# Eight single PSUM banks, first loads on other queues, and v products on GpSimd in a linear-attention and MLP kernel

## The chip, the core and the metric

The kernel runs on one core of a Trainium2 chip. Its time is the device time of one execution in microseconds (us): 360.28 is the median of three runs of the kernel before (359.89, 360.28 and 363.01). The core's engines work side by side, each through its own queue in order: TensorE (PE: matrix products and transposes into PSUM; its weight loads are listed as PEld), VectorE (DVE), ScalarE (ACT), GpSimd (POOL) and SyncE (SP, which here only asks for DMAs). An engine that reaches an instruction whose input is not there stands still, with everything behind it.

## What is computed

```python
def phi(x):                                   # x: 8 batches, 8 heads, 576 rows, 64 columns
    proj = einsum('bhsd,df->bhsf', x, w_phi)  # 128 features
    proj = proj - max(abs(proj), over f)
    return concatenate([exp(proj), exp(-proj)])
kv  = einsum('bhsf,bhsd->bhfd', phi(k), v);  z = sum over s of phi(k)
x   = einsum('bhsf,bhfd->bhsd', phi(q), kv) / (einsum('bhsf,bhf->bhs', phi(q), z) + 1e-6)
x   = x as 4608 rows of 8 heads x 64 = 512 columns
out = square(relu(x @ w_in)) @ w_out          # w_in 512 x 2048, w_out 2048 x 512
```

Inputs and output are float32; the products are made in bf16.

## The kernel before

**Two streams.** For each of 8 batches an attention part makes 4.5 tiles of 128 rows of `x`, 36 tiles in all. An MLP part takes them in chunks (`CHUNKS`: four of one tile, sixteen of two).

**Attention, a batch** (`k_batch`, `q_batch`). Keys are brought in with a cast to bf16, transposed (on PE for the first two batches, L630, by the DMA transpose after that), and projected with `w_phi` (L660) in five groups of 8, 8, 8, 8 and 4 blocks of 128 x 128. Of each group DVE takes the largest absolute value in a row (L595), and ACT makes exp of plus and of minus the projection (L602, tile `kph`). The row's maximum is applied on the side of v: ACT makes exp of it (`em`, L704), and `va` is v times that factor, eight blocks at a time (L755; `var` at L738 for the 64 rows that are left of a batch), with the factor itself as one more column (L716, L720). PE multiplies `kph` with `va` (L776, L781) into `kv`, copied to SBUF as `kvs`. For q there are two projections, one with rows on the partitions for the maximum (L878, reduced at L925) and one transposed (L888), from which ACT makes `qph` (L915). PE then forms numerator and denominator (L970, L978), DVE scales and adds the two halves (`tmp`, L1001 to L1019), takes the reciprocal (L1032) and multiplies (`xo`, L1042, L1046); `xo` is transposed into `xT`.

**MLP, a chunk** (`hp_chunk`, `op_chunk`). `hp` = `w_in` times `xT` (L1133) fills a bank of 512 columns at a time; relu takes it to SBUF (`hr`, L1151 on ACT or L1153 on DVE); it is squared from `hr` into `h2` (L1161 or L1163), one bank per instruction; `w_out` follows (L1189), a copy to `ot` and a DMA to `out`.

**PSUM.** There are 8 banks of 512 float32 columns. Ring `pj` holds three tiles of two banks each (projections, `kv` after the first batch, numerators); ring `mo` holds two single banks (transposes, the first batch's `kv`, `hp` and `op`). One reduction or one exp reads both banks of a `pj` tile: 1024 columns. In `after_kp` a lock keeps the reduction and the exps of the same tile apart in time.

**Order.** Every step is an `Op` with the engines that may do it, a cost, what it needs and what it holds. The table `ORDER`, made ahead of time, lists all steps in the order in which they are issued; a negative entry takes the second engine in the step's list. Each engine works in just that order. `WARM` adds matmuls on the identity ahead of some steps of PE; 24 on zeros (`WARM_UP`) open the kernel, and the step `fill` adds 40 (`FILL`) in the first batch. None of their results is read.

**First loads.** Keys of heads 0, 1, 4 and 5 come as float32 by SP's queue and are cast by ACT and DVE. GpSimd's queue asks, in this order, for the other heads of k, for v, then makes the identity, and asks for the rests of k and v, half of q, two parts of `w_in`, the other half of q, two more parts, the rest of q, batch 1's k, the two halves of `w_out` and batch 1's q and v. `w_phi` comes twice by ACT's queue, for partitions 0 to 63 and 64 to 127, into a tile of two column blocks.

Of the kernel before, what the change touches and what calls it, by code (L numbers as in the profile page):

```python
# [8 lines left out]
F32 = mybir.dt.float32  # L9
# [217 lines left out]
def kernel(  # L227
# [160 lines left out]
    def e_first(op):  # L388
        warm(r_pj.tile(op)[:, 0], WARM_UP, zero)
# [878 lines left out]
```

## Time and profile before

| what | value |
|---|---|
| time, median of three | 360.28 us |
| span of the profiled execution, first to last instruction | 358.4 us |
| its own time | not listed apart; the median stands 1.88 us above the span |
| busy: PE, DVE, ACT, POOL | 346.4, 292.4, 262.9, 58.5 us |
| chain of work that ended last: PE, DVE, ACT | 82%, 8%, 7% |
| mean granted TensorE clock | 0.990 |

The page of the profile has each engine's busy time, the span in 40 slices, and the chain of work that ended last. The table by windows gives the busy time of each engine in chosen stretches with the count of instructions in brackets, and the granted clock of TensorE (1.00 is full). The timeline lists instructions with their start, their length, and the idle time before them with what ended it. The groups by line and shape give the count, the busy time (overlaps counted once), and the mean length of one. Times count from the first instruction.

### The profile page before, as it was taken

The numbers are of one execution on the slowest core, as the hardware profiler recorded it, in microseconds if no ns is written. First come the engines' busy times: TensorE is split into PE (matmuls) and PEld (weight loads), VectorE is DVE, ScalarE is ACT, GpSimd is POOL, SyncE is SP. The second block draws the span as 40 slices with busy tenths as digits, with TensorE's granted clock in tenths as the row PEclk, the third lists the DMA queues.
The fourth block names the chain that finished last, engine by engine and source line by source line (L and its number), as shares of the span: only waits on it lengthen the run. The fifth ranks groups of instructions, "written<-read, shape, count | busy, mean of one in ns | idle before, by whom it ended". The sixth has DMA issues, their size and how long they took to land.

```text
span 358.4 us, 9254 instructions
## 1 busy us (share of the span) xinstructions
PE 346.4 (97%) x3860; PEld 239.1 (67%) x3894; DVE 292.4 (82%) x529; ACT 262.9 (73%) x436; POOL 58.5 (16%) x88
## 2 busy tenths in 40 slices
PE   8699999999999999999999999999999999999995
PEld 4378667775776676767576757757685768576754
DVE  5979998889998998788988699979988988591310
ACT  4979997996798774698849883798879867544641
POOL 8643323442160113100220002000000000000000
PEclk9969999999999999999999999999999999999999
DMA  9999999999997499607982194435203001113011
GB/s 161 185 197 207 194 208 141 170 181 187 186 152 138 83 171 150 107 15 145 124 126 53 59 149 96 61 89 82 60 16 88 18 35 48 65 34 88 2 59 59
DMA packets 92281, 39.33 MB, mean 110 GB/s; under 512 B 59728, under 2 KB 87760, under 8 KB 92240
## 3 DMA queue, kind: packets, MB, share of 16 engines
q0 software_dynamic: 42752, 18.09, 42.7%
q1 hardware_dynamic: 49328, 20.59, 28.6%
q8 instruction: 30, 0.49, 0.6%
q10 hardware_dynamic: 160, 0.07, 0.1%
q14 instruction: 11, 0.09, 0.1%
HBM read 36.77 MB, written 9.44 MB: 129 GB/s over the span
## 4 chain that ended last, share of the span: by engine, by line
PE 82%; DVE 8%; ACT 7%; issue 1%; POOL 1%; ACTq 0%; POOLq 0%
PE mo L1133 32%; PE mo L1189 31%; PE pj L781 4%; PE pj L970 4%; ACT kph L602 4%; PE pj L878 3%; PE pj L888 2%; DVE m L595 2%; PE pj L660 2%; DVE tmp L1009 1%; ACT hr L1151 1%; PE pj L776 1%; PE mo L781 1%; DVE va L755 1%; DVE hr L1153 1%
## 5 line engine op out<-in xcount | busy, mean ns | idle before, releaser
L1133 PE MATMUL mo<-xT,win 128*128 128x256 bf16 (+1 forms) x1280 | 139.3, 262 | 0.8 <-ACT hr L1151 0.2
L1189 PE MATMUL mo<-wout,h 128*128 128x512 bf16 (+1 forms) x558 | 131.2, 373 | 1.8 <-issue 0.2
L1133 PEld LDWEIGHTS <-win 128*128 128x128 bf16 x1280 | 111.3, 98 | 19.7 <-issue 4.3
L1189 PEld LDWEIGHTS <-h 128*128 128x128 bf16 x592 | 54.5, 98 | 57.3 <-issue 2.8
L915 ACT ACTIVATE qph<-pj 128x1024 bf16<-128x1024 f32 (+1 forms) x80 | 72.8, 940 | 11.6 <-PE pj L888 11.6
L1151 ACT ACTIVATE hr<-mo 128x512 bf16<-128x512 f32 x99 | 58.7, 598 | 28.2 <-PE mo L1133 27.0
L602 ACT ACTIVATE kph<-pj 128x1024 bf16<-128x1024 f32 (+1 forms) x80 | 71.2, 949 | 6.4 <-PE pj L660 4.9
L1163 DVE TENSOR_TENSOR h<-hr 128x512 bf16<-128x512 bf16 x82 | 33.7, 419 | 22.6 <-ACT hr L1151 22.0
L925 DVE TENSOR_REDUCE mq<-pj 128x8 f32<-128x1024 f32 (+1 forms) x40 | 44.2, 1108 | 4.5 <-PE pj L878 4.4
L595 DVE TENSOR_REDUCE m<-pj 128x8 f32<-128x1024 f32 (+1 forms) x40 | 44.3, 1111 | 3.4 <-ACT kph L602 1.7
L1161 ACT ACTIVATE h<-hr 128x512 bf16<-128x512 bf16 x62 | 38.9, 631 | 8.3 <-DVE hr L1153 7.5
L755 DVE TENSOR_TENSOR va<-vin,em 128x512 bf16<-128x512 bf16 x63 | 40.2, 683 | 0.1
L1153 DVE TENSOR_SCALAR hr<-mo 128x512 bf16<-128x512 f32 x45 | 30.6, 684 | 7.9 <-PE mo L1133 7.4
L417 ACT ACTIVATE ot<-mo 128x512 f32<-128x512 f32 (+1 forms) x24 | 14.0, 585 | 25.1 <-PE mo L1189 25.1
L1009 DVE TENSOR_TENSOR tmp<-pj,e 128x520 f32<-128x520 f32 x31 | 21.1, 692 | 6.1 <-PE pj L970 6.1
L970 PEld LDWEIGHTS <-qph 128*128 128x128 bf16 x512 | 21.9, 98 | 5.4 <-issue 1.5
L1042 DVE TENSOR_TENSOR xo<-tmp,rden 128x512 bf16<-128x512 f32 (+1 forms) x39 | 24.3, 631 | 0.5
L970 PE MATMUL pj<-kvs,qph 128*128 128x65 bf16 x512 | 24.4, 194 | 0.2
L781 PEld LDWEIGHTS <-kph 128*128 128x128 bf16 x512 | 21.5, 101 | 0.3
L1013 DVE TENSOR_TENSOR tmp<-pj,tmp 128x520 f32<-128x520 f32 x31 | 21.2, 692 | 0.5 <-PE pj L970 0.4
L781 PE MATMUL pj<-va,kph 128*128 128x65 bf16 x448 | 18.4, 194 | 0.0
L467 POOL DMA_DIRECT2D vin<-in_v_dram x8 | 7.2, 895 | 68.5 <-DVE va L755 63.1
(75 smaller groups left out, 268.5 us busy)
## 6 DMA issues: line engine op xcount, KB each, us to landing
out_dram<-ot SPq DMA_DIRECT2D x31, 256.0 KB, 2.4
vin<-in_v_dram POOLq DMA_DIRECT2D x8, 512.0 KB, 9.0
kin<-in_k_dram POOLq DMA_DIRECT2D x7, 512.0 KB, 11.9
qin<-in_q_dram POOLq DMA_DIRECT2D x7, 512.0 KB, 10.3
win<-in_moe_w_in_dram POOLq DMA_DIRECT2D x4, 512.0 KB, 10.1
wout<-in_moe_w_out_dram POOLq DMA_DIRECT2D x2, 1024.0 KB, 14.8
out_dram<-ot SPq DMA_DIRECT2D x10, 128.0 KB, 2.4
xT<-xo SPq DMA_TRANSPOSE x36, 2.6
```

The costliest lines, as they stand in the source:

```text
L595: nc.vector.tensor_reduce(out=st["m"].rearrange("p (n c) -> p c n", c=2)[:, :, n0 : n0 + n], in_=st["pj", g][:, :, :n], axis=AX.X, op=ALU. ...
L602: nc.scalar.activation(out=st["kph"][:, s, n0 : n0 + n].rearrange("p n c f -> p c n f"), in_=st["pj", g][:, :, :n], func=ACT.Exp, scale=1. ...
L755: nc.vector.tensor_tensor(out=st["va"][:, s, gs, 0:D], in0=tiles["v", b].rearrange("p h i d -> p (h i) d")[:, gs, :], in1=st["em"][:, s, g ...
L781: nc.tensor.matmul(out=kv[:, sum_of(h) - 2 * prs[0], :], lhsT=st["kph"][:, s, 2 * h + i // 2, i % 2, :], rhs=st["va"][:, s, h * NI + i, :] ...
L915: nc.scalar.activation(out=st["qph", pt][:, s, half, n0 : n0 + n], in_=in_, func=ACT.Exp, scale=1.0 - 2.0 * s)
L925: nc.vector.tensor_reduce(out=st["mq", pt][:, half, n0 : n0 + n], in_=in_, axis=AX.X, op=ALU.max, apply_absolute_value=True)
L970: nc.tensor.matmul(out=nps[:, n + 4 * (ab or 0), :], lhsT=qph[:, s, half, sl, :], rhs=kvs[:, s, sum_of(sl), :], start=True, stop=True)
L1133: nc.tensor.matmul(out=hp[:, mi, :], lhsT=win[:, kc, mc * P : (mc + 1) * P], rhs=st_x[c][:, kc, 0:nt, :], start=kc == kcs[0] and (ab is No ...
L1151: nc.scalar.activation(out=out_, in_=in_, func=ACT.Relu)
L1153: nc.vector.tensor_scalar(out=out_, in0=in_, scalar1=0.0, scalar2=None, op0=ALU.max)
L1161: nc.scalar.activation(out=out_, in_=hr, func=ACT.Square)
L1189: nc.tensor.matmul(out=st["op"], lhsT=hst["h2"][:, mc, tt * P : (tt + 1) * P], rhs=wout[:, mc, cols], start=(mc == 0), stop=(mc == KC2 - 1))
```

## The change

- **PSUM.** The rings `pj` and `mo` are gone. `r_ps` has eight single banks, for every step. Each projection takes two banks with a `Hold` each; reductions, exps, the additions into `tmp` and the copies of `kv` work on one bank each (512, 256 or 260 columns). In `after_kp` the lock holds one bank instead of two.
- **Counts.** Exps of `kph` and `qph` go from 80 and 80 to 160 and 160, the reductions on DVE from 80 to 160, the additions into `tmp` of full tiles from 62 of 520 columns (and 4 of 260) to 128 of 260.
- **Squares.** `hr` holds two banks, and one instruction squares 1024 columns (in all chunks but the last): ACT has 26 of 1024 and 4 of 512 instead of 62 of 512, DVE 42 and 4 instead of 82. Relus: 82 on ACT and 62 on DVE, instead of 99 and 45.
- **GpSimd.** `va_on` has GpSimd as a second engine, and so has the step of `xo`. In the new table 48 of the 64 products of `va` in all batches and 15 of the 16 of `var` stand on GpSimd, and 19 of the 41 of `xo`. In the first batch these are 6 of the 8 `va` and both `var`; ACT's eight small `va` instructions are gone. The columns of ones are copied by ACT or DVE.
- **First loads.** v of the first batch comes as float32 by SP's queue, in two halves, behind the keys and the rest of k, and stays float32 in a buffer of `h2`. The rest of k is cast by ACT. The identity is made ahead of GpSimd's first DMA. `w_phi` comes with one DMA that reads it twice, into a tile without column blocks. GpSimd's queue: other heads of k, rest of v, half of q, two parts of `w_in`, the other half of q, batch 1's k, two parts of `w_in`; then the eight products of the first batch; then the rest of q, batch 1's rest of k, the two halves of `w_out`, batch 1's q and v.
- **Later loads.** From batch 3 on they wait, on GpSimd, for a small copy from the first `xo` of the batch two before (`load_gate`, tile `mark`).
- **Fillers.** The 40 matmuls of `fill` are gone; `WARM` has other places, with 42 instead of 57.
- **Order.** A new table for 2084 steps instead of 1718.

The core of the diff, without the two tables and the changes of names:

```diff
-    r_pj = Ring("pj", 3, [P, 2, 4, P], F32, pool=ps)
-    r_mo = Ring("mo", 2, [P, 4, P], F32, pool=ps)
+    r_ps = Ring("ps", 8, [P, 4, P], F32, pool=ps)
-    r_hr = Ring("hr", 4, [P, 512], BF16)
+    r_hr = Ring("hr", 3, [P, 2, 512], BF16)
...
     def c_wst(_):
-        for half in range(2):
-            nc.scalar.dma_start(out=wst[half * Dh : (half + 1) * Dh], in_=w_phi)
+        nc.scalar.dma_start(out=wst, in_=w_phi.unsqueeze(0).to_broadcast([2, Dh, Fd]))
...
+            def emit_v(op, n=n):
+                if n == 0:
+                    tiles["v", 0] = r_h2.tile(op, [P, H, NI, D], dtype=F32)
+                nc.sync.dma_start(out=tiles["v", 0].rearrange("p h i d -> p h (i d)")[:, 4 * n : 4 * n + 4],
+                                  in_=v[0, 4 * n : 4 * n + 4, 0:SM, :].rearrange("h (p i) d -> p h (i d)", i=NI))
...
-            lock = Lock()
...
+            for par in range(2):
+                lock = Lock()
...
-        if b == 0:
-
-            def e_fill(op):
-                warm(r_mo.tile(op), FILL)
...
-            va_on = {"dve": (0.6, 0.69)}
+            va_on = {"dve": (0.6, 0.69), "pool": (1.0, 1.05)}
...
-                        nc.vector.tensor_tensor(
+                        eng = nc.gpsimd if op.engine == "pool" else nc.vector
+                        eng.tensor_tensor(
                             out=st["va"][:, s, gs, 0:D],
...
-                    o_xo = add(ks - 2.4, {"dve": dve(64 * (nh if ab is None else 4))}, e_xo, [o_rd],
+                    o_xo = add(ks - 2.4, {"dve": dve(n)} if first_tile else {"dve": dve(n), "pool": pool(n)}, e_xo, [o_rd],
...
-            def e_sq(op, mcs=mcs):
-                hr = st["hr", mcs[0]]
-                out_ = st["h2"][:, mcs[0] : mcs[-1] + 1, 0 : nt * P]
+            def e_sq(op, m0=m0, m1=mcs[-1] + 1, n=len(o_hrs)):
+                hr = st["hr", m0][:, :n].rearrange("p a (m t) -> p (a m) t", m=gm)
+                out_ = st["h2"][:, m0:m1, 0 : nt * P]
...
+    def load_gate(b, key):
+        o_xo, owner, st, name = firsts[b - 2]
+
+        def emit(_):
+            nc.gpsimd.tensor_copy(out=mark[:, b : b + 1], in_=st[name][:, 0, 0:1])
+
+        return add(key, {"pool": (0.1, 0.12)}, emit, [o_xo], give=[(r_xo.slots, owner)])
```

More of the change, by code (lines that the diff above doesn't have):

```diff
@@ L264 @@
     EARLY = 2
-    XB_IN, XB_X = 2, 2
+    XB_IN, PE_X = 2, [(b, pt, half) for b in range(2) for pt in range(3) for half in range(2)]
     def sum_of(h):
@@ L369, in c_w2 @@
     def c_w2(op):
-        for half in range(2):
-            rows = slice(half * Dh, (half + 1) * Dh)
-            copy(op, w2[rows, half], wst[rows])
+        copy(op, w2, wst)
     def c_wst(_):
-        for half in range(2):
-            nc.scalar.dma_start(out=wst[half * Dh : (half + 1) * Dh], in_=w_phi)
+        nc.scalar.dma_start(out=wst, in_=w_phi.unsqueeze(0).to_broadcast([2, Dh, Fd]))
     def c_var(_):
@@ L417, in copy @@
             nc.scalar.activation(out=out_, in_=in_, func=ACT.Copy)
+        elif op.engine == "pool":
+            nc.gpsimd.tensor_copy(out=out_, in_=in_)
         else:
@@ new lines, in k_batch, with e_kp @@
+        for g in groups:
+            key = kd - 6.0 - 2.2 * (4 - g)
+            holds = [Hold(r_ps.slots) for _ in range(2)]
+            def e_kp(op, g=g, holds=holds):
+                if g == 0:
+                    st["kph"], st["m"] = r_kph.tile(op), r_m.tile(op)
+                n0, n = GROUPS[g]
+                pj = [r_ps.tile(hold) for hold in holds]
+                st["pj", g, 0], st["pj", g, 1] = pj
+                warm(pj[0], op.warm)
+                for u in range(n):
+                    for par in range(2):
+                        rows = slice(par * Dh, (par + 1) * Dh)
+                        nc.tensor.matmul(out=pj[par][:, u, :], lhsT=st["kT"][rows, n0 + u, :], rhs=w2[rows, :],
+                                         start=True, stop=True)
+            o_kp = add(key - 1, {"pe": mm(P, GROUPS[g][1])}, e_kp, [cp_ops[g], o_w2],
+                       holds + ([r_kph.slots, r_m.slots] if g == 0 else []),
@@ L877, in e_qm @@
                             rows = slice(par * Dh, (par + 1) * Dh)
[L878 to L879 removed]
+                            nc.tensor.matmul(out=pj[bank][:, u, :], lhsT=q_blocks(st, pt, blk + u, 1)[rows, 0],
+                                             rhs=w2[rows, :], start=True, stop=True)
                 def e_qp(op, pt=pt, pi=pi, mms=mms, w=w, hq=hq):
[L882 removed]
+                    pj = st["pq", pt, pi] = [r_ps.tile(hold) for hold in hq]
@@ L907, in q_batch @@
-                if split and pi:
-                    late = o_qm, o_qp
-                o_mq, o_q0 = o_mq or o_qm, o_q0 or o_qp
-                for s in range(2):
-                    def e_exp(op, pt=pt, pi=pi, half=half, n0=n0, n=n, w=w, s=s):
-                        in_ = st["pq", pt, pi][:, :, :w]
-                        if n == 8:
-                            in_ = in_.rearrange("p a b t -> p (a b) t")
-                        nc.scalar.activation(out=st["qph", pt][:, s, half, n0 : n0 + n], in_=in_, func=ACT.Exp,
-                                             scale=1.0 - 2.0 * s)
-                    exps.setdefault(pi, []).append(add(key + 2.5 + 0.2 * s, {"act": act(size)}, e_exp, [o_qp],
-                                                       give=[(r_pj.slots, hq)]))
@@ L921, in e_red @@
-                def e_red(op, pt=pt, pi=pi, half=half, n0=n0, n=n, w=w):
-                    in_ = st["pm", pt, pi][:, :, :w]
-                    if n == 8:
-                        in_ = in_.rearrange("p a b t -> p (a b) t")
-                    nc.vector.tensor_reduce(out=st["mq", pt][:, half, n0 : n0 + n], in_=in_, axis=AX.X, op=ALU.max,
-                                            apply_absolute_value=True)
-                reds.append(add(key + (3.5 if b == 0 else 0.5), {"dve": dve(size)}, e_red, [o_qm], give=[(r_pj.slots, hm)]))
+                o_qm = add(key, {"pe": mm(P, w * (1 + split))}, e_qm, need + [o_w2], hm + first[:1], give=qT_give,
+                           after=[o_mq], mode="row")
@@ new lines, in q_batch, with e_exp, e_red @@
+                o_qp = add(key + (0.1 if b else 2), {"pe": mm(128 * w, 1 + split)}, e_qp, need + [o_w2], hq + first[1:],
+                           give=qT_give, after=[o_q0], mode="row")
+                o_mq, o_q0 = o_mq or o_qm, o_q0 or o_qp
+                mine = []
+                for bank, (half_, h0, nh_) in enumerate(banks):
+                    for s in range(2):
+                        def e_exp(op, pt=pt, pi=pi, bank=bank, half_=half_, h0=h0, nh_=nh_, w=w, s=s):
+                            nc.scalar.activation(out=st["qph", pt][:, s, half_, h0 : h0 + nh_],
+                                                 in_=st["pq", pt, pi][bank][:, :w], func=ACT.Exp, scale=1.0 - 2.0 * s)
+                        exps[half_, h0, s] = add(key + 2.5 + 0.2 * s, {"act": act(128 * w)}, e_exp, [o_qp],
+                                                 give=[(r_ps.slots, hq[bank])])
+                    def e_red(op, pt=pt, pi=pi, bank=bank, half_=half_, h0=h0, nh_=nh_, w=w):
+                        nc.vector.tensor_reduce(out=st["mq", pt][:, half_, h0 : h0 + nh_], in_=st["pm", pt, pi][bank][:, :w],
+                                                axis=AX.X, op=ALU.max, apply_absolute_value=True)
+                    mine.append(add(key + (3.5 if b == 0 else 0.5), {"dve": dve(128 * w)}, e_red, [o_qm],
+                                    give=[(r_ps.slots, hm[bank])]))
@@ new lines, in q_batch @@
+                            give = [(r_ps.slots, hold) for hold in holds]
+                            if s == 0:
+                                give.append((r_e2.slots, e2s[0]))
+                            at = ab or hg
+                            o_t[at] = add(ks - 3.5 + 0.5 * s, {"dve": dve(260) if pt < 2 else (0.85, 0.95)},
+                                          e_t, [o_nd, o_e2, o_t.get(at)], [] if o_tmp else [r_tmp.slots], give=give,
+                                          after=[o_tmp])
```

362 lines of the change are left out of this document (169 added, 193 removed), and 191 rows, old and new, of the table ORDER.

## The prediction

> **What bounds the kernel now.** I read the page first (busy times), then the table by windows, then the timeline of the start, the groups by shape, and the DMA issues. The page, and the table for the stretches before and after the first MLP matmul (28.41 us); its columns are PE, PEld, DVE, ACT and POOL with counts in brackets, then the granted clock:
>
> ```profile
> PE 346.4 (97%) x3860; PEld 239.1 (67%) x3894; DVE 292.4 (82%) x529; ACT 262.9 (73%) x436; POOL 58.5 (16%) x88
> ```
> ```profile
> 0.00:28.40 28.40, 23.21 (x250) 14.72 (x250) 22.40 (x45) 20.27 (x44) 18.25 (x32) 0.88 1.29 182
> 28.40:54.00 25.60, 24.86 (x357) 18.36 (x356) 25.38 (x49) 24.11 (x46) 7.95 (x11) 1.00 1.42 203
> 54.00:81.00 27.00, 26.37 (x373) 19.65 (x375) 22.56 (x43) 23.31 (x37) 11.28 (x16) 1.00 1.51 164
> 81.00:108.00 27.00, 26.79 (x328) 17.94 (x326) 26.34 (x44) 20.83 (x34) 8.25 (x12) 1.00 1.37 175
> 108.00:351.00 243.00, 241.42 (x2537) 165.44 (x2562) 195.75 (x352) 173.00 (x277) 12.77 (x18) 1.00 0.44 79
> 351.00:358.40 7.40, 3.76 (x34) 3.04 (x31) 0.00 (x0) 1.36 (x3) 0.00 (x0) 0.98 0.19 71
> ```
>
> TensorE is the bound. From 28.4 to 108 it is idle for 0.74 + 0.63 + 0.21 = 1.58 us, and from 108 to 351 for 1.58 of 243, at full clock. Faster work of any other engine there is worth 3.2 us at most, and the new program has the same matmuls, fillers apart. The end (from 351) is not touched. So the time is decided ahead of 28.4: whatever brings PE's dense stream forward moves the whole rest with it, as long as the inputs of that stream follow. The start:
>
> ```profile
> 3.62 0.42 ACT L417 ACTIVATE kin<-h 128x256 bf16<-128x256 f32 x1 [0.37 <-DMA h<-in_k_dram]
> 5.11 0.31 ACT L417 ACTIVATE w<-wst 64x128 bf16<-64x128 f32 x1 [0.87 <-DMA wst<-in_w_phi_dram]
> 5.73 0.42 DVE L419 COPY kT<-mo 128x512 bf16<-128x512 bf16 x1 [1.67 <-PE mo L630]
> 6.67 0.40 PE L660 MATMUL pj<-w,kT 64*128 64x128 bf16 x8
> 7.11 1.23 DVE L595 TENSOR_REDUCE m<-pj 128x8 f32<-128x1024 f32 x1 [0.75 <-PE pj L660]
> 8.36 2.85 ACT L602 ACTIVATE kph<-pj 128x1024 bf16<-128x1024 f32 x3 [0.34 <-DVE m L595]
> 9.07 2.33 PE L400 MATMUL mo<-ident 128*128 128x512 bf16 x10
> 11.09 0.33 ACT L704 ACTIVATE em<-m 128x16 f32<-128x16 f32 x2
> 17.14 0.67 ACT L602 ACTIVATE kph<-pj 128x512 bf16<-128x512 f32 x1
> 17.62 2.07 ACT L750 ACTIVATE va<-vin,em 128x64 bf16<-128x64 bf16 x8
> 19.52 2.00 ACT L915 ACTIVATE qph<-pj 128x1024 bf16<-128x1024 f32 x2
> 22.67 0.65 PE L781 MATMUL mo<-va,kph 128*128 128x65 bf16 x8
> 24.72 0.39 ACT L417 ACTIVATE kvs<-mo 128x260 bf16<-128x260 f32 x1 [0.88 <-PE mo L781]
> 28.41 1.79 PE L1133 MATMUL mo<-xT,win 128*128 128x128 bf16 x29
> ```
> ```profile
> 15.00:16.66 1.66, 0.00 (x0) 0.00 (x1) 1.62 (x4) 1.66 (x5) 1.00 (x3) 1.00 1.35 196
> 16.66:23.70 7.04, 7.04 (x82) 5.84 (x83) 6.00 (x10) 5.58 (x19) 3.25 (x5) 0.52 1.40 199
> ```
>
> The first exp waits until 8.36, although its projection began at 6.67: the lock lets it start only when DVE has reduced both banks (7.11 to 8.34). From there ACT's pieces follow each other to 21.52, the end of the first two `qph`. PE has nothing to do from 15.00 to 16.66, after which it runs at 0.52 of its clock until 23.70, busy all the time: kv is late because PE is slow there. The last `kvs` copy ends at 25.11, and 3.3 us later the MLP begins.
>
> **The change, part by part.** Lengths by shape:
>
> ```profile
> L602 ACT ACTIVATE kph<-pj 128x1024 bf16<-128x1024 f32 x64 | 62.9, 1034 | 6.4 <-PE pj L660 4.9 <-DVE m L595 1.3
> L602 ACT ACTIVATE kph<-pj 128x512 bf16<-128x512 f32 x16 | 9.2, 607 | 0.0
> L595 DVE TENSOR_REDUCE m<-pj 128x8 f32<-128x1024 f32 x32 | 38.8, 1218 | 3.4 <-ACT kph L602 1.7 <-PE pj L660 1.2
> L595 DVE TENSOR_REDUCE m<-pj 128x4 f32<-128x512 f32 x8 | 5.5, 683 | 0.1
> L1009 DVE TENSOR_TENSOR tmp<-pj,e 128x520 f32<-128x520 f32 x31 | 21.1, 692 | 6.1 <-PE pj L970 6.1
> L1001 DVE TENSOR_TENSOR tmp<-pj,e 128x260 f32<-128x260 f32 x2 | 0.8, 422 | 0.6 <-PE pj L970 0.6
> L755 DVE TENSOR_TENSOR va<-vin,em 128x512 bf16<-128x512 bf16 x63 | 40.2, 683 | 0.1
> L738 DVE TENSOR_TENSOR var<-vrest,em 64x512 bf16<-64x512 bf16 x16 | 11.0, 685 | 1.3 <-ACT em L704 1.0
> L1161 ACT ACTIVATE h<-hr 128x512 bf16<-128x512 bf16 x62 | 38.9, 631 | 8.3 <-DVE hr L1153 7.5
> L1151 ACT ACTIVATE hr<-mo 128x512 bf16<-128x512 f32 x99 | 58.7, 598 | 28.2 <-PE mo L1133 27.0
> L720 POOL CAST var<-em 64x8 bf16<-64x8 f32 x2 | 0.4, 214 | 1.1 <-ACT em L704 1.0
> ```
>
> *Evacuation by single banks.* An exp of 1024 columns takes 62.9/64 = 0.98 us of ACT, one of 512 9.2/16 = 0.575. Splitting 128 of them costs 2 x 0.575 - 0.98 = 0.17 each, 21 us; the 32 smaller ones add some 0.1 each, 3 us. Against it stand 17 relus fewer (58.7/99 = 0.59 each, -10 us) and squares merged: 26 of 1024 columns at about 0.98 and 4 at 0.63 are 28 instead of 38.9 us. ACT stays within 5 us of 263. On DVE, splitting 64 reductions costs 2 x 0.69 - 1.21 = 0.17 each, 11 us, the 62 additions 2 x 0.4 - 0.68 = 0.12 each, 7 us, and 17 relus come in; but 47 `va` (40.2/63 = 0.64 each, 30 us), 15 `var` (11.0/16 = 0.69, 10 us) and 19 `xo` leave it: DVE gets some 20 us lighter. Both have room beneath PE after 28.4, so I cost this at nothing there. If that cover fails, 5 us of ACT work in the full stretch 28.4 to 54 (24.11 of 25.60 busy) would cost some 3.
>
> *Start, up to the first exp.* `w_phi` needs one landing; before, the second copy ran only at 5.11. The keys land at the same 3.6; three casts on ACT (0.42 each, overlapping), the transposes and their copy (0.42 before) put the projection at about 5.45 instead of 6.67, and its end half a us later. ACT then takes the second bank while DVE reduces the first. First exp: 5.95 instead of 8.36, -2.4 us.
>
> *ACT's chain to qph.* From 8.36 to 19.52 before. The sixteen exps of 512 and four of 256 need about 0.8 more than the ten before; new on ACT are the cast of k's rest (0.4) and four copies of ones (0.2 each, like `em`, 0.33 for two); gone are the eight `va` (2.07); I add 0.8 for waits on DVE's reductions. So 19.52 - 2.4 + 0.8 + 0.4 + 0.8 - 2.07 + 0.8 = 17.85.
>
> *GpSimd's products.* No product on GpSimd is in the trace. From below: its 64x8 cast takes 0.21, so a product is over that, say 0.5 with 64 times the columns. From above: twice DVE's 0.68, and one collision with a DVE product of 0.68: 2.05. I take the 1.05 that the kernel's own table of costs has, since the same table has 0.6 to 0.69 for DVE's `va`, and the trace 0.68. The first factor `em` comes after nine exps and the cast, 5.95 + 4.45 = 10.4; product one until 11.45, the second needs the rests' factor (about 12.05), the eight end at 12.05 + 7 x 1.05 = 19.4. The last kv (0.65 at half clock, twice) then ends at about 20.9, ahead of the ACT instruction that copies it, so they are hidden behind ACT. [...]
>
> *First MLP matmul.* From 17.85 ACT has two exps, `e`, a `kvs` copy, five exps and the last `kvs` copy: 7 x 0.575 + 0.2 + 2 x 0.39 = 5.0, less 0.5 for overlap back to back: 22.3, instead of 25.11. Then the old 3.3, less 0.4 for the first half's additions that no longer stand behind it: 25.2. That is -3.2. If PE is again at half clock in this stretch (the 40 fillers that kept it busy from 9.07 to 11.40 are gone), the few matmuls between are inside those 2.9. [...] Bounds: 23.5 if GpSimd and PE never make it wait (-4.9), and 27.5 if ACT's chain gains nothing beyond the first exp's lead less its new work (-0.9).
>
> *More done by then.* The new order has 12 transposes, 2 matmuls of 512 columns more and 8 of 65 fewer ahead of the first MLP matmul. At 1.79/29 = 0.062 for 128 columns: 12 x 0.062 + 8 x 0.062 - 8 x 0.031 = 1.0 us, -1.0.
>
> *After 28.4.* Of the 1.37 us that PE is idle to 81 I take half back, -0.7, since DVE, which is full there (25.38 of 25.60), loses products to GpSimd.
>
> *What is late next: `w_out`.*
>
> ```profile
> L477 POOL DMA_DIRECT2D krest<-in_k_dram x16 | 10.1, 639 | 12.5 <-DMA kT<-krest 5.8 <-DMA qin<-in_q_dram 4.8 <-DMA win<-in_moe_w_in_dram 0.9
> 19.93 0.89 POOL L531 DMA_DIRECT2D wout<-in_moe_w_out_dram  x1 [0.90 <-DMA qin<-in_q_dram]
> 22.52 0.88 POOL L531 DMA_DIRECT2D wout<-in_moe_w_out_dram  x1 [1.69 <-DMA win<-in_moe_w_in_dram]
> DMA to landing us min/median/max: 13.4/14.8/16.1
> L1189 PE MATMUL mo<-wout,h x37: 379/379/390, 40.1 to 57.1; 128*128 128x512 bf16 x37
> ```
>
> It is now queued on GpSimd behind the eight products and four small issues (0.64 each): 19.4 + 2.6 = 22.0 instead of 19.93. It lands 13.4 to 16.1 later, 35.4 to 38.1. PE's first use of it stands 11.2 us of matmuls behind the first MLP matmul: 25.2 + 11.2 = 36.4. Between a gain of nothing and a stall of 1.7 I take +0.8. Batch 1's q and v are queued behind it and slip with it by about 2 us; what hides that is the MLP work of the first chunks, and if it does not, those 2 us are the price. Squares over two banks make `h2` ready up to a relu and half a square later (0.9 us); four to eight banks in flight hide that.
>
> *Sum.* -3.2 - 1.0 - 0.7 + 0.8 = -4.1: a span of 354.3, and with the 1.9 by which the median (360.28) stands above the profiled span (358.4), 356.2 us.
>
> **Rivals.** *ACT eats the lead (same).* ACT is on the path from 8.4 to 21.5 without a gap, and it gets 2 us of new work there. If splitting ten exps costs the whole 0.17 each, and PE's clock drops earlier because the fillers are gone, kv ends where it did; the MLP starts at 27.5, less 1.0 for the work done ahead, plus a late `w_out`: 358.5 to 360. For it: the half clock came after a PE gap of under 2 us; against it: the waits of the lock are gone for sure. I take 359.
>
> *GpSimd becomes the chain (slower).* With products of p us the eight end at 10.4 + 8p or so, kv 1.5 later, the MLP 3.9 after that as now. Up to p = 1.5 the start is no later than 28.4; from there each 0.1 costs 0.8, and `w_out`, issued 2.6 after them, slips as much. At p = 2.05 the products end at 26.8 and the MLP starts at 32.2: +3.8, less 1.0, with 1.0 for `w_out` (landing at 44 on the mean, used at 43.4) and 1.0 for waits of later batches: 358.4 + 4.8 + 1.9 = 365.1 us. For it: nothing in the trace shows a product there, and DVE works in SBUF beside it all the time. Against it: ACT and DVE are planned around 1.05.
>
> **How the numbers follow.** Forecast (356.2, own range 353 to 357.5): 0.58. ACT eats the lead (359): 0.25. GpSimd the chain (365): 0.17. A measurement of this kernel tells about 1%, 3.6 us, from no change. Faster by more is below 356.7: the forecast less 0.04 for its upper tail, 0.54. Slower is above 363.9: the last rival less 0.03 for products that only just pass 1.5, 0.14. Same is the rest: 0.04 + 0.25 + 0.03 = 0.32. The range goes from 353.0 (start at 23.5: 358.4 - 4.9 - 1.0 - 1.4 and no late `w_out`, + 1.9) to 362.0, which leaves out most of the last rival and a little of the forecast below.
>
> **What would show it.** Right: first exp of `kph` near 6.0; the first MLP matmul at 24 to 26; PE over 97% busy behind it; GpSimd's products near 1.05; the first `w_out` matmul waiting less than 2 us. Wrong: products over 1.5, kv waiting for POOL, PE waiting for DMAs of batch 1, or an ACT that is the releaser of most PE waits beyond 28.

## The result, and the profile after

The changed kernel takes 381.7 us (median of four runs, 379.4 to 382.39) against 360.08 of the kernel before on the same chip: a ratio of 1.0575, 95% interval 1.053 to 1.062, 21.6 us slower. The prediction was 356.2 with a range to 362. The profiled execution of the changed kernel took 382.39 us, with a span of 380.6 (before: 358.4).

The page of the changed kernel (busy times, the granted clock in 40 slices, the chain of waits):

```profile
PE 353.7 (93%) x3888; PEld 244.9 (64%) x3888; DVE 284.8 (75%) x566; ACT 257.0 (68%) x559; POOL 145.8 (38%) x170
PEclk9669997999999999699999999999999999999999
PE 60%; DVE 20%; DMA 7%; ACT 5%; issue 3%; SPq 2%; POOL 1%; DVEq 0%; ACTq 0%; POOLq 0%
```

DVE's share of the chain went from 8% to 20% and DMA now has 7%, although DVE is busy 7.6 us less. Two slices in the middle show a clock of 6 and 7 tenths, where the kernel before had none. The table by windows, of the changed kernel and then of the kernel before (columns as in the prediction):

```profile
54.00:81.00 27.00, 23.16 (x324) 16.99 (x324) 21.98 (x47) 19.53 (x45) 12.93 (x18) 0.87 0.63 90
130.00:160.00 30.00, 25.73 (x267) 15.85 (x266) 17.62 (x38) 15.70 (x36) 12.44 (x17) 0.91 1.08 148
28.40:380.60 352.20, 331.56 (x3652) 230.21 (x3650) 263.80 (x527) 237.55 (x509) 122.30 (x138) 0.98 0.61 97
```
```profile
28.40:358.40 330.00, 323.20 (x3613) 224.43 (x3644) 270.03 (x485) 242.61 (x393) 40.25 (x57) 1.00 0.67 104
```

Behind 28.4 us PE is idle for 352.2 - 331.56 = 20.6 us, before for 6.8. That is 13.8 of the 22.2 us by which the span grew. The other 8.4 us are longer busy time. Two stretches of 6.8 us at a granted clock of 0.50 make up 5.6 of it by an estimate that takes half of the 5.12 and 6.14 us that PE is busy in them (a matmul of 256 columns took 0.22 us of busy time from 154.65 to 161.48, 0.13 from 162 to 175 at full clock); the rest would be work of the start, whose first MLP matmul comes 1.8 us later.

```profile
55.67:62.49 6.82, 5.12 (x41) 3.22 (x41) 5.86 (x12) 1.79 (x5) 3.13 (x3) 0.50 0.77 147
154.65:161.48 6.83, 6.14 (x28) 3.78 (x28) 1.29 (x2) 5.17 (x11) 0.00 (x0) 0.50 1.26 203
```

These stretches are those of one execution. The four executions had mean granted clocks of 0.963, 0.976, 0.977 and 0.987 and took 382.39, 381.76, 379.4 and 381.64 us, so the time hardly followed the clock, and what the half rate costs is open.

Ahead of the first stretch stands one gap of PE. The timeline of the changed kernel there:

```profile
51.27 1.05 POOL L781 TENSOR_TENSOR va<-vin,em 128x512 bf16<-128x512 bf16 x1 [4.08 <-ACT em L730]
51.32 1.05 DVE L438 CAST va<-em 128x16 bf16<-128x16 f32 x1
52.26 3.06 DVE L438 CAST var<-em 64x8 bf16<-64x8 f32 x2
52.26 0.95 POOL L511 DMA_DIRECT2D vin<-in_v_dram  x1
53.22 1.05 POOL L763 TENSOR_TENSOR var<-vrest,em 64x512 bf16<-64x512 bf16 x1
53.51 0.40 PE L1092 MATMUL ps<-ident,xo 128*128 128x128 bf16 x4
54.23 1.04 POOL L781 TENSOR_TENSOR va<-vin,em 128x512 bf16<-128x512 bf16 x1
55.44 1.54 DVE L781 TENSOR_TENSOR va<-vin,em 128x512 bf16<-128x512 bf16 x1
56.90 0.41 DVE L438 COPY qT<-ps 128x512 bf16<-128x512 bf16 x1
57.37 1.87 PE L1213 MATMUL ps<-wout,h 128*128 128x512 bf16 x4 [3.46 <-DVE qT L438]
```

Three casts of a few columns take DVE from 51.32 to 55.32, while GpSimd makes products and, from 52.26 on, issues a DMA. The chain of waits has the last of them by itself:

```profile
52.44 2.88 DVE var L438
```

This one cast lasts until GpSimd has ended the two products that follow the DMA's issue. Behind the casts in DVE's queue stands the copy of `qT` for which PE waits 3.46 us (53.91 to 57.37), and 1.8 us into that gap the clock drops. The groups by shape, changed kernel first, then the kernel before:

```profile
L781 POOL TENSOR_TENSOR va<-vin,em 128x512 bf16<-128x512 bf16 x42 | 47.1, 1143 | 40.2 <-ACT em L730 24.7 <-issue 14.7 <-DMA vin<-in_v_dram 0.5
L781 DVE TENSOR_TENSOR va<-vin,em 128x512 bf16<-128x512 bf16 x14 | 12.3, 888 | 0.7 <-issue 0.6
L438 DVE CAST var<-em 64x8 bf16<-64x8 f32 x6 | 5.4, 898 | 0.0
L438 DVE CAST va<-em 128x16 bf16<-128x16 f32 x5 | 3.4, 683 | 0.0
L438 DVE CAST va<-em 128x64 bf16<-128x64 f32 x2 | 2.2, 1089 | 0.0
```
```profile
L720 DVE CAST var<-em 64x8 bf16<-64x8 f32 x14 | 2.7, 194 | 0.1
L716 DVE CAST va<-em 128x64 bf16<-128x64 f32 x6 | 1.8, 303 | 0.0
L716 DVE CAST va<-em 128x16 bf16<-128x16 f32 x8 | 1.5, 236 | 0.0
```

The same casts take 194 to 303 ns before and 683 to 1089 after. So the first theory: a GpSimd product and a DVE instruction that works in SBUF alone keep each other out ("the lock" from here on, not the one in `after_kp`); DVE, which works in order, passes the delay on to PE, and the fixed order has no slack for it. The rivals: the new table with its single banks is slow by itself (theory 2, later rival 1); or DMAs land late (theory 3).

### The profile page after: what moved, and what is told of

Read it like the earlier page. It is cut to its first block, busy times and chain, and to the rows that moved or that the text cites. A ratio compares the mean times of both kernels' runs of the same rounds, so it can differ in the third digit from the quotient of the medians.

```text
span 380.6 us, 9564 instructions
## 1 busy us (share of the span) xinstructions
PE 353.7 (93%) x3888; PEld 244.9 (64%) x3888; DVE 284.8 (75%) x566; ACT 257.0 (68%) x559; POOL 145.8 (38%) x170
## 3 DMA queue, kind: packets, MB, share of 16 engines
q0 software_dynamic: 41168, 17.50, 38.9%
## 4 chain that ended last, share of the span: by engine, by line
PE 60%; DVE 20%; DMA 7%; ACT 5%; issue 3%; SPq 2%; POOL 1%; DVEq 0%; ACTq 0%; POOLq 0%
PE ps L1142 26%; PE ps L1213 20%; PE ps L804 4%; DMA xT<-xo 4%; PE ps L978 3%; DVE m L634 3%; DVE tmp L1013 2%; ACT kph L642 2%; DMA qin<-in_q_dram 2%; DVE mq L929 2%; SPq L1077 2%; DVE hr L1170 2%; DVE tmp L1020 2%; PE ps L898 2%; DVE h L1186 2%
## 5 line engine op out<-in xcount | busy, mean ns | idle before, releaser
L1142 PE MATMUL ps<-xT,win 128*128 128x256 bf16 (+1 forms) x1280 | 141.2, 266 | 5.5 <-DMA xT<-xo 3.6
L1213 PE MATMUL ps<-wout,h 128*128 128x512 bf16 (+1 forms) x592 | 135.5, 375 | 4.9 <-DVE qT L438 3.5
L922 ACT ACTIVATE qph<-ps 128x512 bf16<-128x512 f32 (+1 forms) x160 | 79.5, 570 | 16.1 <-PE ps L908 16.0
L642 ACT ACTIVATE kph<-ps 128x512 bf16<-128x512 f32 (+1 forms) x160 | 79.5, 573 | 10.0 <-PE ps L699 8.1
L1168 ACT ACTIVATE hr<-ps 128x512 bf16<-128x512 f32 x82 | 48.7, 604 | 32.8 <-PE ps L1142 25.8
L1170 DVE TENSOR_SCALAR hr<-ps 128x512 bf16<-128x512 f32 x62 | 41.7, 682 | 28.5 <-PE ps L1142 27.9
L781 POOL TENSOR_TENSOR va<-vin,em 128x512 bf16<-128x512 bf16 x42 | 47.1, 1143 | 40.2 <-ACT em L730 24.7
L634 DVE TENSOR_REDUCE m<-ps 128x4 f32<-128x512 f32 (+1 forms) x80 | 47.8, 627 | 5.6 <-ACT kph L642 3.7
L929 DVE TENSOR_REDUCE mq<-ps 128x4 f32<-128x512 f32 (+1 forms) x80 | 46.8, 626 | 5.8 <-PE ps L898 5.5
L1186 DVE TENSOR_TENSOR h<-hr 128x1024 bf16<-128x1024 bf16 (+1 forms) x46 | 33.7, 735 | 8.3 <-ACT hr L1168 7.7
L434 ACT ACTIVATE ot<-ps 128x512 f32<-128x512 f32 (+1 forms) x22 | 13.0, 589 | 28.4 <-PE ps L1213 22.0
L804 PEld LDWEIGHTS <-kph 128*128 128x128 bf16 x512 | 21.6, 101 | 1.6 <-issue 1.4
```

Of the source, the lines that this page charges most:

```text
L634: nc.vector.tensor_reduce(out=st["m"].rearrange("p (n c) -> p c n", c=2)[:, par, n0 : n0 + n], in_=st["pj", g, par][:, :n], axis=AX.X, op= ...
L642: nc.scalar.activation(out=st["kph"][:, s, n0 : n0 + n, par, :], in_=st["pj", g, par][:, :n], func=ACT.Exp, scale=1.0 - 2.0 * s)
L781: eng.tensor_tensor(out=st["va"][:, s, gs, 0:D], in0=tiles["v", b].rearrange("p h i d -> p (h i) d")[:, gs, :], in1=st["em"][:, s, gs].uns ...
L804: nc.tensor.matmul(out=kv[:, sum_of(h) - 2 * prs[0], :], lhsT=st["kph"][:, s, 2 * h + i // 2, i % 2, :], rhs=st["va"][:, s, h * NI + i, :] ...
L922: nc.scalar.activation(out=st["qph", pt][:, s, half_, h0 : h0 + nh_], in_=st["pq", pt, pi][bank][:, :w], func=ACT.Exp, scale=1.0 - 2.0 * s)
L929: nc.vector.tensor_reduce(out=st["mq", pt][:, half_, h0 : h0 + nh_], in_=st["pm", pt, pi][bank][:, :w], axis=AX.X, op=ALU.max, apply_absol ...
```

## The experiments

The kernel before ran beside each group of these: 359.8 to 360.9 us. Each fence of a diff shows the core of an edit.

**The lock by itself.** A small kernel of its own, in three stretches: DVE and ACT instructions alone, GpSimd's products alone, and both.

```diff
+    for _ in range(100):
+        product(0)          # GpSimd, 128 x 512, float32 factor broadcast
+    for _ in range(8):
+        nc.vector.tensor_copy(out=ones[:, :, 64], in_=em[:, 0:16])
...
```

> None of the reference's work is done; the output is zeros. Eight each of nine kinds of DVE instruction and two of ACT, first alone, then beside a row of 100 GpSimd products of 128 x 512 (float32 factor broadcast, bf16 out), with eight of these alone between. Theory 1: beside GpSimd the DVE kinds that read and write SBUF alone (casts of ones, va product, squares) get up to one GpSimd product longer (the casts from 0.2 to about 1 us), or GpSimd's products get longer in their turn; those that read PSUM (relu, reductions, kT copies, additions to tmp) stay as they are, and so do ACT's. Rival (the casts were long in the changed kernel for another reason, such as a wait that the trace puts into the length): all kinds within 10% of their length alone.

Its groups; the smaller line number of each pair is the kind alone:

```profile
L63 DVE CAST ones<-em 128x16 bf16<-128x16 f32 x8 | 1.6, 202 | 0.2
L98 DVE CAST ones<-em 128x16 bf16<-128x16 f32 x8 | 8.7, 1086 | 0.2
L65 DVE TENSOR_TENSOR va<-vin,em 128x512 bf16<-128x512 bf16 x8 | 5.6, 694 | 0.2
L100 DVE TENSOR_TENSOR va<-vin,em 128x512 bf16<-128x512 bf16 x8 | 10.6, 1322 | 0.2
L67 DVE TENSOR_TENSOR h<-hr 128x1024 bf16<-128x1024 bf16 x8 | 5.5, 692 | 0.2
L102 DVE TENSOR_TENSOR h<-hr 128x1024 bf16<-128x1024 bf16 x8 | 11.4, 1428 | 0.2
L73 DVE TENSOR_SCALAR relu<-bank 128x512 bf16<-128x512 f32 x8 | 5.5, 690 | 0.2
L108 DVE TENSOR_SCALAR relu<-bank 128x512 bf16<-128x512 f32 x8 | 5.5, 690 | 0.2
L80 ACT ACTIVATE relua<-banka 128x512 bf16<-128x512 f32 x8 | 4.8, 597 | 0.3
L114 ACT ACTIVATE relua<-banka 128x512 bf16<-128x512 f32 x8 | 4.8, 595 | 0.2
```

The casts of 16 columns get 0.88 us longer, products and squares 0.63 and 0.74, each less than one GpSimd product alone (1.12). Everything that reads PSUM (relus 690 ns in both, reductions 689 and 690, copies 423 and 422, additions 426 and 427), ACT (597 and 595, squares 1055 and 1056), and a reciprocal in float32 (202 ns in both) stay as they were. GpSimd's products take 1.28 us each while DVE's instructions run beside them, 1.12 ahead of that and 1.02 behind it, with DVE idle. Theory 1's mechanism is there, in that both sides take longer. What it is that the two share, no run shows; `port`, in the kernel a mark of steps of `va`, `var`, `xo` and the squares, is no more than a name for it.

**The products back on DVE, order kept.**

```diff
+            if o.engine == "pool" and "dve" in o.engines:   # all; or va and var only; or xo only
+                o.engine = "dve"
```

> The changed kernel with all 82 products of va, var and xo on DVE; the order table, the eight banks and the loads stay. DVE gets 48 x 0.64 + 15 x 0.69 + 12 x 0.68 + 7 x 0.42 = 52 us of work more. Theory 1 (a GpSimd product and a DVE instruction that works in SBUF alone keep each other waiting, and DVE's queue then holds up PE): the casts of ones fall from 0.9 to 0.2 us, the half clock at 55 and 154 us is gone, and the time is 360 to 368, although DVE has 52 us more. Theory 2 (the single banks and the new order are to blame, the products' engine is not): DVE is only fuller, 382 to 392. Theory 3 (late DMAs: the transposes of xo at 150 us, v and w_phi at the start): 376 to 384, with the wait of 6.5 us on xT still there.

> The changed kernel with the 63 products of va and var on DVE, xo's 19 still on GpSimd. Theory 1: the stall of 3.5 us at 52 us and its half clock go, as the casts and var were the instructions held up there; 366 to 374. Theory 2: 380 to 390. Theory 3: as now, 378 to 384.

> The changed kernel with the 19 products of xo on DVE, va and var still on GpSimd. Theory 1: xo's products are 18 of GpSimd's 89 us of products, so a fifth of the loss goes at most: 374 to 381; if the chain through xo and its transposes at 120 to 160 us is what counts, 370. Theory 2: 381 to 386. Theory 3: 378 to 384.

Measured: 428.7, 418.9 and 404.4 us (ratios 1.193, 1.163, 1.121, each within 0.008). All far outside what the theories expected. Theory 1 is wrong in one part: to clear GpSimd is no cure while the table stays. DVE is busy 315.2, 306.8 and 295.6 us instead of 284.8, that is 30, 22 and 11 more, and the kernel takes 47, 37 and 23 more. In this order a microsecond added to DVE costs about 1.5 to 2.1 (the added work stands net of the lock that goes). The table was made for GpSimd's products running beside DVE. If it has no room for these products, it has none either for what the lock adds; that is an inference, which the later experiments test.

**Idle products in the kernel before.** This separates the lock from the table: nothing moves, GpSimd only makes products that nobody reads.

```diff
+                        if b >= 2: dummy(st["em"][:, s, gs])
...
+        nc.gpsimd.tensor_tensor(out=scratch["b"], in0=scratch["a"], in1=em.unsqueeze(2).to_broadcast([P, 8, D]), op=ALU.mult)
```

> The kernel before with nothing moved, but beside each of DVE's 48 va products of batches 2 to 7 GpSimd makes a product of the same shape from the same factor into a tile that nobody reads. [...] Theory 1: DVE's va and casts get longer by up to 0.6 each beside it, 20 to 30 us in sum; DVE has some 45 us of room from 108 to 351, so the time grows by 3 to 20: 363 to 380. Rival 1 (the lock is real but a queue absorbs it): 359 to 362.

> The kernel before with the same 48 idle GpSimd products of batches 2 to 7, each over one column in 64 (8 elements a row instead of 512, about 0.25 us). The control for the 47 us that the full ones cost: same instructions, waits on em and releases of em, but little time in the port. Theory 1 (the lock): the loss shrinks nearly with the length, 359 to 368. Rival (a GpSimd reader of em holds buffers or delays DMA issues): 385 or more.

Measured: 408.1 us (ratio 1.132, 1.127 to 1.137) with full products, 361.6 (1.003, 1.0005 to 1.005) with one column in 64. Groups of the first:

```profile
L581 POOL TENSOR_TENSOR dummyb<-dummya,em 128x512 bf16<-128x512 bf16 x48 | 59.8, 1246 | 148.8 <-ACT em L706 145.9
L757 DVE TENSOR_TENSOR va<-vin,em 128x512 bf16<-128x512 bf16 x63 | 56.1, 935 | 0.7 <-DMA vin<-in_v_dram 0.5
L740 DVE TENSOR_TENSOR var<-vrest,em 64x512 bf16<-64x512 bf16 x16 | 18.8, 1176 | 1.3 <-ACT em L706 1.0
L718 DVE CAST va<-em 128x64 bf16<-128x64 f32 x6 | 7.5, 1252 | 0.0
```

And its table of PE's waits (us in total, times, longest):

```profile
PE pj L779 <- DVE var L740: 6.8, 1, 6.8
PE mo L1136 <- DVE hr L1156: 6.6, 1, 6.6
```

DVE's own `va` went from 40.2 to 56.1 us, `var` from 11.0 to 18.8, the casts of 64 columns from 1.8 to 7.5; DVE is 38.9 us busier in all, and PE waits up to 6.8 us at a time for it. The kernel is 47 us longer, where at most 20 had been expected, for work that no step needs, and nearly all of that goes when the products are short. So the lock costs time in the old order too; it needs no new table.

**What the lock is worth in the changed kernel.** GpSimd's products cut to one column in 64 (`va` and `var`; then `xo` too), and the casts of ones moved to ACT.

```diff
-                            out=st["va"][:, s, gs, 0:D],
+                            out=st["va"][:, s, gs, 0:1 if op.engine == "pool" else D],
...
+            if op is a copy of ones:   # the other experiment
+                o.engine = "act"
```

> The changed kernel, engines and order untouched, but the 63 products of va and var on GpSimd write one column of 64 (the other 63 keep what a memset at the start, 2 us on DVE, put there), so 63 parts in 64 of those products are left out; a product falls from 1.14 to some 0.2 us. In the measured run the DVE kinds that work in SBUF alone were some 17 us longer in sum than alone (casts of ones 8, va 3, squares 3, xo 2, var 1). Theory 1 as it stands now (in this table DVE's queue has no room: 10.8 us more of DVE work cost 22 us with xo on DVE, 22 us cost 37 with va and var there; GpSimd's lock adds some 15 us to DVE): most of the 15 go, and the time falls to 355 to 366. Rival 1 (the table and the single banks are bad by themselves, whatever GpSimd does): 375 to 384. Rival 2 (it is the length of GpSimd's products that kv waits for, not the lock): also 355 to 366, but then the casts on DVE are no shorter in it than now.

> The changed kernel with all 82 products on GpSimd, xo's too, cut to one column in 64 (the rest left out), and the tiles behind them filled once at the start. With va and var cut it was 372. If the 18 us of xo's products, in the port and on the path from tmp to the transposes, are what is left: 362 to 367. If what is left is the table itself (single banks, more instructions, transposes too close to their use): 369 to 373.

> The changed kernel with the casts of the ones columns (13 on DVE, 11.0 us there, 0.9 each instead of 0.2) on ACT, which the single measurement shows untouched by GpSimd; ACT gets 13 x 0.25 = 3.3 us. Theory 1: DVE is 11 us lighter, at 1.3 or more per us: 364 to 372, and the PE gap at 57 us shrinks or goes. Rival 1: 378 to 386, since ACT is no emptier than DVE.

Measured: 372.3 us (ratio 1.034, 1.031 to 1.037), 371.9 (1.031, 1.027 to 1.034) and 375.5 (1.043, 1.039 to 1.047). The first and the third lie between the ranges of theory 1 and rival 1, the second in that of the table itself. The products of `va` and `var` cost 9.4 of the 21.6 us, those of `xo` nothing (by the intervals such a difference is good to about 2 us). Moving thirteen small casts to ACT alone brings 6.2, and the gap at 57 us goes with them: PE is busy 26.38 us from 54 to 81 instead of 23.16. That the casts shrink with the products (the 64 x 8 ones to 204 ns) speaks for the lock and against mere length. But some 12 us stay, so rival 1 or the DMAs have a part.

**The loads of a batch beside transposes.** In the changed kernel, and also with the products cut or the casts on ACT, PE stood still, and then ran at half clock, between 140 and 162 us (3.7, 3.6 and 3.9 us of waiting for a copy into `ot`, a granted clock of 0.91, 0.89 and 0.89 from 130 to 160).

```diff
-            nc.gpsimd.tensor_copy(out=mark[:, b : b + 1], in_=st[name][:, 0, 0:1])   # no gate
...
+            if (name, b) == ("k", 5): nc.gpsimd.tensor_copy(out=mark[:, 0:2], in_=st_x[8][:, 2, 1, 0:128:64])   # late5
```

> The changed kernel without the small copy that holds back the loads of batches 3 to 7; they go as soon as GpSimd's queue and the input buffers let them. In every variant so far two transposes of xo at about 140 us and the output DMA between them take 6 to 8 us to land, while GpSimd, released by that copy at 138 us, has just asked for k, the rests and q of a batch; PE stands still for 3.7 us there and loses some 3.4 us more at half clock. Theory 4 (the gate bunches the loads onto those transposes; a second cause beside the lock): 372 to 377. Rival (the transposes are late anyway, or the loads only collide elsewhere): 380 to 386.

> The ones columns on ACT and no gate, together; the whole computation is done. If the two causes add up: 375.5 less 5 to 8: 367 to 371. If the gate is not a cause: 374 to 379.

> Products of va and var on GpSimd cut to one column in 64 (63 parts in 64 of them left out), and no gate. If the lock and the gate are the two causes of the loss, what is left is xo's 18 us on GpSimd and the start: 362 to 367. If something else of the table (single banks, squares) is behind the rest of the loss: 370 to 374.

Measured: 383.7, 378.7 and 375.8 us, 2 to 3.5 more than with the gate in each case. This experiment could not decide: without the gate batch 5's k was still asked for at the same moment (138.5 us against 138.9, in the pair with cut products). Ahead of it in GpSimd's queue stands a product of `xo`, which itself starts only at 137.72 after 16.61 us of waiting. So the edit took away a wait that was not the last one, and told nothing about the meeting of loads and transposes. The next edit holds the loads until the transposes have landed.

> As with va and var cut to one column (372.3; 63 parts in 64 of these products are left out), and batch 5's loads, asked for at 138 us, held until both transposes of the rest tile of xo have landed (a copy of two elements of that tile on GpSimd ahead of them). If the transposes land late because the loads share the DMA engines with them: they land in 3 to 4 us instead of 6 to 7, the wait of 3.6 us at 147 and the half clock behind it go, 364 to 368, unless batch 5's keys are then late. If they are late without the loads: 371 to 375.

> The ones columns on ACT (375.5) and the same hold on batch 5's loads; the whole computation is done. If the loads delay the transposes: 367 to 371. If not: 374 to 378.

> The changed kernel with nothing but the hold on batch 5's loads until the transposes of the rest tile of xo have landed. With the ones columns on ACT, and with va and var cut, the hold gave 3.0 and 4.0 us. If it stands by itself beside the lock: 377 to 380 for the changed kernel. If the lock shifts the meeting of loads and transposes: 381 to 384.

Measured: 368.3 us (ratio 1.021, 1.018 to 1.024), 372.5 (1.032, 1.027 to 1.038) and 377.4 (1.047, 1.044 to 1.051): 4.0, 3.0 and 4.3 us less than without the hold. The first two lie between the ranges set for them, the third in the range of a cause beside the lock. The timelines of GpSimd, SP and PE, changed kernel and then with the hold:

```profile
145.69 0.94 POOL L511 DMA_DIRECT2D kin<-in_k_dram  x1
148.11 3.15 SPq L1077 DMA_TRANSPOSE xT<-xo  x2
155.22 0.61 PE L908 MATMUL ps<-qT,w 64*128 64x512 bf16 x2 [3.72 <-ACT ot L434]
```
```profile
147.32 2.45 SPq L1078 DMA_TRANSPOSE xT<-xo  x2
150.93 0.19 POOL L509 COPY mark<-xT 128x2 bf16<-128x2 bf16 x1 [5.99 <-DMA xT<-xo]
```

The chain of waits of the changed kernel there, and the window from 130 to 160 with the hold:

```profile
150.04 6.49 DMA xT<-xo
156.56 3.57 PE ps L1142 x16
```
```profile
130.00:160.00 30.00, 29.68 (x352) 20.28 (x350) 22.85 (x51) 20.57 (x45) 10.58 (x15) 1.00 0.85 127
```

Beside the loads a transpose lands 6.5 us after its issue ended, and PE goes on with it at 156.56. The gap of 3.72 us just ahead is for a copy into `ot`, whose buffer an output DMA still held; with the products cut, the chain of waits names the one that SP had issued between the transposes, 6.8 us long. With the hold both have landed at 150.93, when the copy that waits for them starts, 1.2 us after the second was issued (147.32 + 2.45). PE is then busy 29.68 of 30 us at full clock from 130 to 160, instead of 25.73 at 0.91. So the loads here delay what lands beside them (6.5 us against 1.2), and that is a second cause beside the lock. Part of the gain is given back later (PE is busy 36.91 us from 160 to 200 instead of 39.22, with 1.5 us of waiting for the rest of k, which now comes later).

**Instructions split over single banks**, in the kernel before, with its order.

```diff
-                nc.vector.tensor_reduce(... in_=st["pj", g][:, :, :n], ...)
+                for c in range(2): nc.vector.tensor_reduce(... in_=st["pj", g][:, c, :n], ...)   # exps and tmp likewise
```

> The kernel before with its own order and rings, but each exp, each reduction and each addition into tmp that reads two banks made as two instructions, one for each bank, as in the change. DVE gets 64 x 0.17 + 62 x 0.12 = 18 us, ACT 64 x 0.17 + 64 x 0.17 + 3 = 24 us. If there is room beneath PE for that, as the prediction had it: 360 to 363. If every us on DVE or ACT in these fixed orders costs about one (48 idle products made DVE 39 us longer and the kernel 47): 375 to 395.

> The kernel before with exps, reductions and additions into tmp split over single banks in batches 1 to 7 only; the first batch as it was. Split everywhere it was 365.3, 4.8 over the kernel before, with the first MLP matmul at 29.70 instead of 28.41 and 3.4 us more at half clock ahead of it. If the cost is that of the start: 360 to 361.5. If it lies in the full stretch behind it, where DVE and ACT get some 38 us more: 363 to 366.

Measured: 365.3 us (ratio 1.012, 1.009 to 1.015) and 364.0 (1.010, 1.007 to 1.014). So the split costs 4.8 us, of which 3.9 remain when the first batch is left alone. The prediction had it hidden, which it is not, but it is far cheaper than the lock: 39 us more on DVE cost 47, 7.8 on DVE (292.4 to 300.2) and 8.6 on ACT (262.9 to 271.5) cost 4.8. The 18 and 24 us of more work that the prediction counted came out at less than half.

**`w_phi` in one landing**, alone, in the kernel before.

```diff
-        for half in range(2):
-            nc.scalar.dma_start(out=wst[half * Dh : (half + 1) * Dh], in_=w_phi)
+        nc.scalar.dma_start(out=wst, in_=w_phi.unsqueeze(0).to_broadcast([2, Dh, Fd]))
```

> The kernel before with w_phi brought in by one DMA that reads it twice, everything else as it was. The second copy of it into the weights tile ran at 5.11 us, 0.87 after ACT was free for it. By the prediction's first step that copy goes to 4.3 and the first projection up to 0.8 us earlier: 359.3 to 360. If the keys of the second DMA (about 5.4 us) set the first exps anyway: 360 to 361.

Measured: 360.18 us, ratio 0.999 (0.997 to 1.001). No difference. The one landing comes later than the two did:

```profile
5.88 0.64 ACT L416 ACTIVATE w<-wst 64x128 bf16<-64x128 f32 x2 [1.98 <-DMA wst<-in_w_phi_dram]
```

ACT waits until 5.88 for it (before, the second copy ran at 5.11), and the first exp is at 8.25 instead of 8.36. Why the one landing is later, no run shows.

## Why the prediction was wrong

The step that failed is "Both have room beneath PE after 28.4, so I cost this at nothing there", with "DVE gets some 20 us lighter" and "-0.7" behind it: instead of -0.7, PE is idle 13.8 us longer behind 28.4. A second term failed too, the start: 25.2 was forecast for the first MLP matmul, and it ran at 30.24, which is 5.0 of the 25.5 us between forecast and result. What the experiments give:

| part of the 21.6 us | measured by | us |
|---|---|---|
| `va`, `var` on GpSimd | products cut to a column | 9.4 |
| `xo` on GpSimd | those cut as well | 0.4 |
| batch 5's loads beside the transposes of `xo` | loads held | 4.3 |
| `va`, `var` and the loads together | cut and held | 13.4 |
| left with both gone | 368.3 - 360.1 | 8.2 |

Of the 8.2, splitting over banks may be 4.8, as it was in the kernel before; that was not tried in the new table, where it can't be undone without a new order. Late landings have a part as well: in that run PE still waits 7.8 us for DMAs (3.6 for transposes of `xo`, 1.9 for q of the first batch, 1.8 for the rest of k, 0.5 for keys), and in the kernel before its list of waits has no DMA. How the 8.2 divide between these, the squares over two banks and the table itself stays open.

*After 28.4.* DVE did get lighter, but by 7.6 us instead of 20, since the lock lengthened what was left: with `va` and `var` cut to a column DVE is busy 271.0 us, 21.4 less than before. So the sum of DVE's own work was about right, and what was missing is the lock. Added up from the groups, thirteen casts cost 11.0 us instead of 3.0, and fourteen `va` 12.3 instead of 9.6. ACT came out at 257.0, near the "within 5 us of 263". Wrong was to read the room of an engine off its busy share. DVE works in order and PE waits for particular instructions of it, so a delay of 3 us in one place is a gap of 3.46 us in PE, and in the profiled execution a stretch at half clock behind it, however empty DVE is elsewhere.

*Products on GpSimd.* The 1.05 us was right: 1.03 to 1.05 where DVE does not hold it up, 1.12 in the small kernel, and 1.14 on the mean. The collision with DVE stood in the text, as an upper bound for GpSimd ("one collision with a DVE product of 0.68"), whose "twice DVE's 0.68" was the author's estimate (alone the products took 1.02 to 1.12, DVE's 0.69); its other side, that DVE is held up, did not. In the first batch the products ended at 21.99 instead of 19.4: the first began at 12.30 instead of 10.4, and the last three took 4.02 us with DVE's casts and products between them. Hidden behind ACT they were not, as PE waits 1.28 us for a cast of ones that comes late with them:

```profile
17.97 4.02 POOL L781 TENSOR_TENSOR va<-h,em 128x512 bf16<-128x512 f32 x3
18.96 2.13 DVE L781 TENSOR_TENSOR va<-h,em 128x512 bf16<-128x512 f32 x2
21.01 1.04 DVE L438 CAST va<-em 128x16 bf16<-128x16 f32 x1
22.10 0.60 PE L804 MATMUL ps<-va,kph 128*128 128x65 bf16 x8 [1.28 <-DVE va L438]
```

But they are at most a small part of what made kv late. Its last matmuls of the first batch end at 26.87 instead of 20.9, and with the products cut to a column still at 25.85.

*Start.* The first exp came at 6.96, not 5.95:

```profile
5.54 0.42 ACT L434 ACTIVATE kin<-h 128x256 bf16<-128x256 f32 x1 [1.24 <-DMA h<-in_k_dram]
6.96 1.65 ACT L642 ACTIVATE kph<-ps 128x512 bf16<-128x512 f32 x3 [0.52 <-PE ps L699]
```

"The keys land at the same 3.6" holds for the first of two DMAs only. The second set is read at 5.54; before, ACT cast its half at 5.43 without a wait, and the first exp stood behind the reduction until 8.36 anyway. A later wait of PE is one that the prediction has no term for, the first half of q:

```profile
12.98 0.40 PE L862 MATMUL ps<-ident,qin 128*128 128x128 bf16 x4 [1.36 <-DMA qin<-in_q_dram]
```

It was asked for at 4.27 and landed 8.7 us later, and the chain of work that ended last runs through it. Behind it in PE's queue stand the last four transposes of k in this batch. PE was also at half clock for 13.7 us ahead of the first MLP matmul (7.88 to 11.29 and 14.70 to 24.95), before for 6.8. With the products cut that matmul ran at 29.21 instead of 30.24, but in the run with nothing but batch 5's loads held, whose start is unchanged, it ran at 29.23 as well, so the 1 us tells nothing of the products. What the wait for q and the half clock cost was not tried apart.

*`w_out`.* Issued at 24.41, 2.4 later than predicted, and PE never waited for it: its first matmul followed at 41.47 with no wait, as the MLP itself was late. The +0.8 was not needed.

*Rivals.* The one that ended on the slow side had GpSimd as the chain, with products over 1.5 us. They are 1.05, and POOL has 1% of the chain of waits. The kernel did get slower, but by a mechanism that no rival named. No version of the changed kernel here beats the kernel before; the best that does all of the work (ones on ACT, loads held) takes 372.5.

## What to carry to other kernels

Before moving elementwise work from VectorE to GpSimd, list which VectorE instructions will run beside it: in the small kernel casts, products and squares that read and write SBUF took 0.39 to 0.88 us longer each beside GpSimd's products, a cast of 16 columns 1086 ns instead of 202, while what read PSUM (a relu 690 in both) and a reciprocal in float32 (202 in both) stayed as they were; in the changed kernel one cast lasted until two products had ended (2.88 us). Price a move by what stands behind the delayed instruction in its queue, not by the engine's busy share. Test a wait by taking away the one that ends last: a gate removed while another step of the same queue waits just as long tells nothing.

## What the runs showed of the hardware that was not expected

- A cast of 8 columns took 170 ns alone, 556 beside GpSimd's products; the products themselves took 1.12 us alone and 1.28 beside them (8 in 8.92 us, 22 in 28.05). Both sides paid.
- In the profiled execution of the changed kernel the clock fell to half 1.8 us after PE stopped (53.91 to 55.67) and stayed there for 6.82 us; at the start for 3.41 and 10.25. What sets the drop and the length of a stay, no run shows.
- With batch 5's loads held, the two transposes had landed 1.2 us after their issue ended; without, one took 6.5, when the loads had been asked for 2.4 us ahead of their issue.
